# Attention over a long cache on one core: ScalarE's sums in a loop over quarter blocks, VectorE's sums twelve keys at a time

## The chip, the cores and the metric

The kernel runs on one core of one Trainium2 chip. The metric is the device time of one execution in microseconds, median of three runs. The program uses five engines: TensorE (PE, matrix products), VectorE (DVE), ScalarE (ACT), GpSimd (POOL, at the start alone) and SyncE (SP, which issues nearly all loads), and the 16 DMA engines that bring the caches from HBM.

## What is computed

One decoding step: one query token, 16 heads of width 256, and caches of 65536 keys and values per head in bf16. The caches are 1074 MB of the 1084 MB that are read. Cut to what matters:

```python
xn = _layernorm(x)                       # x: [1, 1, 448]
q = (xn @ wq) as [16 heads, 256]
scores = einsum("bhqd,bhkd->bhqk", q, k_cache) * 256 ** -0.5
p = softmax(scores)
o = einsum("bhqk,bhkd->bhqd", p, v_cache)
s = o as [1, 4096] @ wo
g = silu(silu(xn @ w1) @ w2)
out = x + s * g
```

## The kernel before

A head's cache is cut into 4 blocks; a block is 128 keys on each of 128 partitions, 32768 bf16 numbers (64 KB) per partition, 8.39 MB in all. There are 64 blocks. Three buffers R[0], R[1], R[2] take them in turn: the keys of block i are loaded, multiplied by the query in place, and when their scores are copied out, the values of the same block are loaded over them.

```python
KB = 128          # keys per partition in a block
SUB = 32          # a quarter block
ND = 19           # keys of a quarter that VectorE sums; ScalarE sums the other NA = 13
NR = 3
...
R = [pool.tile([P, KW], bf16, name=f"R{t}") for t in range(NR)]
...
def take(e, s, k=1):                      # wait for a semaphore, and count it down
    e.wait_ge(s, k).then_inc(s, -k)
...
def load_k(i, s, h=None):
    if h is not None:
        take(sp, h)                       # TensorE is done with half of the old values
    take(sp, vf[s])                       # ... and with all of them
    sp.dma_start(out=R[s][:, :], in_=block(Kd, i)).then_inc(kl[s], 16)
    sp.sem_inc(kq[s], 16)
    sp.sem_inc(kh[s], 16)

def load_v(i, s):
    take(sp, kf[s])                       # the scores of this block are copied out
    sp.dma_start(out=R[s][:, :], in_=block(Vd, i)).then_inc(vl[s], 16)
```

VectorE multiplies ScalarE's 13 keys of a quarter in one instruction, then does its own 19 by a fused multiply-and-sum each. After four quarters it copies the scores and takes their maximum.

```python
def dve_block(s, between=None):
    def end(c0, c1, own):
        take(dve, pf, (c1 - c0) // SUB)   # ScalarE's quarters are done
        take(dve, sd, own)
        dve.tensor_copy(out=S2[:, c0:c1], in_=S[:, c0:c1]).then_inc(kf[s], 1)
        dve.reduce_max(out=rmax[:, :], in_=S[:, c0:c1], axis=AX.X).then_inc(rm, 1)
        if c0 == 0 and between:
            between()
        dve_gmax()
    take(dve, qr)
    dve.tensor_copy(out=qcur[:, :], in_=ps_q).then_inc(sd, 1)
    halves = between is not None          # the last block: two halves, each with a maximum
    take(dve, kl[s], 16)
    for k in range(NSTEP):                # NSTEP = 4
        ...
        m = dve.tensor_tensor(out=pair, in0=pair, in1=qcur[...broadcast...], op=ALU.mult)
        m.then_inc(mr, 1)
        for j in range(ND):
            c = k * SUB + j
            ins = dve.tensor_tensor_reduce(out=Kv[:, c, :], in0=Kv[:, c, :], in1=qcur[:, :],
                op0=ALU.mult, op1=ALU.add, accum_out=S[:, c : c + 1], ...)
        ...
```

ScalarE adds up the products by an identity activation with an accumulator, keeps the outputs of an earlier block between the second and the third quarter, and does the exponentials. Its loop has a body of three blocks, written out.

```python
def act_sums(s, k):
    take(act, mr)
    for j in range(NA):
        c = k * SUB + ND + j
        prod = R[s][:, c * Dh : (c + 1) * Dh]
        ins = act.activation(out=prod, in_=prod, func=ACT.Identity, accum_out=S[:, c : c + 1])
    ins.then_inc(pf, 1)

def act_block(i, s):
    for k in range(NSTEP):
        if k == NSTEP // 2:
            act_keep(i - 2)               # waits for the products of values two blocks back
        act_sums(s, k)
    act_softmax(i, s)                     # exp into PV[s]
```

TensorE takes the row maximum across partitions, then multiplies the weights by the values of the block before:

```python
def pe_block(i, s):
    pe_turn()
    pe_max(i)
    pe_v(s)
```

The three engines' loops begin at a fixed place of an instruction block (`addr_align`, slot 128 for VectorE and ScalarE, 0 for TensorE and SyncE) and carry a hint for the branch back. The last block is written out behind the loops; there the last values and wo are loaded in pieces.

Of the kernel before, what the change touches and what calls it, by code (L numbers as in the profile page):

```python
# [7 lines left out]
ACT = mybir.ActivationFunctionType  # L8
# [5 lines left out]

KB = 128
SUB = 32
ND = 19
NR = 3


@with_exitstack
def kernel(
# [28 lines left out]
    N1 = H1 * NB  # L51
    NL = NENT - N1
    NSTEP = KB // SUB
    NA = SUB - ND
    DF = D // P
    assert D == DF * P + P // 2
    HP = H // 2
# [13 lines left out]

    KW, HK = KB * Dh, KB // 2

    R = [pool.tile([P, KW], bf16, name=f"R{t}") for t in range(NR)]
    qcur = pool.tile([P, Dh], bf16, name="qcur")
    q8 = pool.tile([HP, 2 * Dh], bf16, name="q8")
    S = pool.tile([P, KB], fp32, name="S")
    S2 = pool.tile([P, KB], fp32, name="S2")
    PV = [pool.tile([P, KB], bf16, name=f"PV{t}") for t in range(NR)]
    rmax = pool.tile([P, 1], bf16, name="rmax")  # L80
    gmax = pool.tile([1, 1], bf16, name="gmax")
    O = pool.tile([2, 2 * Dh], fp32, name="O")
# [61 lines left out]
    def mark(e, ins):  # L144
        count[e] += 1
        ins.then_inc(line[e], 1)
        return (e, count[e])
# [7 lines left out]
    def sem(name):  # L155
        return tc.alloc_semaphore(name)

    def take(e, s, k=1):
        e.wait_ge(s, k).then_inc(s, -k)  # L159
# [11 lines left out]
    rm, tm, gm, bm, pv = sem("rm"), sem("tm"), sem("gm"), sem("bm"), sem("pv")  # L171
    od, oc, ho = sem("od"), sem("oc"), sem("ho")
    sd, sa = sem("sd"), sem("sa")
    dl = {n: sem(f"dl_{n}") for n in ("x", "wq", "w1", "w2", "out")}

    def cuts(*c):
# [47 lines left out]
        dve.reduce_max(out=gmax[0:1, :], in_=ps_m[0:1, :], axis=AX.X).then_inc(gm, 1)  # L224


    def dve_block(s, between=None):
        Kv = R[s][:, :].rearrange("p (c d) -> p c d", d=Dh)


        def end(c0, c1, own):
            take(dve, pf, (c1 - c0) // SUB)
# [4 lines that stand above are left out]
                between()  # L237
            dve_gmax()

        take(dve, qr)  # L240
        dve.tensor_copy(out=qcur[:, :], in_=ps_q).then_inc(sd, 1)  # L241
        halves = between is not None
        take(dve, kl[s], 16)
        for k in range(NSTEP):
            if k == 1:
                take(dve, kq[s], 16)
            if k == NSTEP // 2:
                take(dve, kh[s], 16)
            pair = Kv[:, k * SUB + ND : (k + 1) * SUB, :]
            m = dve.tensor_tensor(  # L250
                out=pair,
                in0=pair,
                in1=qcur[:, None, :].to_broadcast([P, NA, Dh]),
                op=ALU.mult,
            )
            if k == 0:
                m.wait_op(sd, 1, "sem-ge")
            m.then_inc(mr, 1)
            for j in range(ND):
                c = k * SUB + j  # L260
                ins = dve.tensor_tensor_reduce(  # L261
                    out=Kv[:, c, :],
                    in0=Kv[:, c, :],
                    in1=qcur[:, :],
                    scale=1.0,
                    scalar=0.0,
                    op0=ALU.mult,
                    op1=ALU.add,
                    accum_out=S[:, c : c + 1],
                )  # L270
            if k == NSTEP - 1:
                ins.then_inc(sd, 1)
                end(KB // 2 if halves else 0, KB, 1 if halves else 2)
            elif halves and k == NSTEP // 2 - 1:
                ins.then_inc(sd, 1)
                end(0, KB // 2, 2)

    def act_sums(s, k):
        take(act, mr)
        for j in range(NA):  # L280
            c = k * SUB + ND + j
            prod = R[s][:, c * Dh : (c + 1) * Dh]
            ins = act.activation(  # L283
                out=prod,
                in_=prod,
                func=ACT.Identity,
                accum_out=S[:, c : c + 1],
            )
        ins.then_inc(pf, 1)

    def act_softmax(e, s, c0=0, c1=KB):
        def col(a, b):
            return hist[:, at(e + 2), a:b].rearrange("p o s -> p (o s)")

        take(act, bm)
        act.mul(out=col(0, 1), in_=ps_nb, mul=-scale).then_inc(sa, 1)  # L296
        take(act, sa)
        act.activation(  # L298
            out=PV[s][:, c0:c1],
            in_=S2[:, c0:c1],  # L300
            func=ACT.Exp,
            bias=col(0, 1),
            scale=scale,
            accum_out=col(1, 2),
        ).then_inc(pv, 1)
# [5 lines left out]
    def act_keep(e):  # L311
        act_out()
        return act_row(e)

    def act_row(e):
        take(act, ho)
        return act.copy(out=hist[:, at(e + 2), 2:4].rearrange("p o s -> p (o s)"), in_=ps_t)  # L317


    def act_block(i, s):  # L320
        for k in range(NSTEP):
            if k == NSTEP // 2:
                act_keep(i - 2)
            act_sums(s, k)
        act_softmax(i, s)


    def pe_keys(po, t, s, k0, k1, start, stop, done=None):
# [77 lines left out]

    def loop(g, a, b, step, block, more=0, slot=0):
        es, name = {g.engine}, f"passes_{nc.next_id()}"  # L410
        head, ann, body, rest, join, tail = (
            f"{name}_{x}" for x in ("head", "ann", "body", "rest", "join", "tail")
        )
        assert (b - a) % step == 0 and more < step
        last = b if more else b - step
        r = nc.alloc_registers(f"{name}_i", engines=es)
        nc.regs_mov(r, a)
        g.addr_align(bass.FETCH_BLOCK_INSTRUCTIONS, offset=slot, max_nops=0)
        nc.br(head, engines=es)

        def go(lo, hi):
            i = nc.snap(r, min_val=a, max_val=last)
            for s in range(lo, hi):
                block(i + s, s)

        with nc.body(head, valid_engines=es):
            g.br_eq(r, last, on_true=body, on_false=ann)
        with nc.body(ann, valid_engines=es):
            hint = g.mark_branch_hint_location()
            nc.br(body, engines=es)  # L430
        with nc.body(body, valid_engines=es):
            go(0, more or step)
            if more:
                g.br_eq(r, last, on_true=join, on_false=rest)
            else:
                nc.br(join, engines=es)
        if more:
            with nc.body(rest, valid_engines=es):
                go(more, step)
                nc.br(join, engines=es)  # L440
        with nc.body(join, valid_engines=es):
            nc.regs_alu(r, r, step, op=mybir.AluOpType.add)
            g.br_lt(r, last + 1, on_true=head, on_false=tail).branch_hint(hint)
        nc.switch_bb(tail)

    with tc.tile_critical():

        act.dma_start(out=x_f[0:1, :], in_=A_x[0, 0:1, :]).then_inc(dl["x"], 16)
        load_rows(w1_t, B_w1, F, dl["w1"])
# [164 lines left out]
        for s in range(1, NR):  # L614
            load_k(NR + s, s, vh[s])
            load_v(NR + s - 1, s - 1)
        with nc.Fori(2 * NR, LAST - 2, NR, engines={ET.SP}, head_slot={ET.SP: 0}) as i:
            for s in range(NR):
                load_k(i + s, s, vh[s])
                load_v(i + s - 1, (s - 1) % NR)  # L620
# [23 lines left out]
        load_wo(4)  # L644


        loop(dve, 0, LAST, NR, lambda i, s: dve_block(s), slot=128)
        loop(act, 0, LAST, NR, act_block, slot=128)


        def none(p):
# [8 lines left out]
        none(ps_t2).then_inc(ho, 1)  # L660
        need("pe", t9)
        pe_max(0)
        loop(pe, 1, NBLK - 3, NR, pe_block, more=1)
        pe_turn()
        pe_v(1, 96, lambda: pe_max(NBLK - 2))


        def weights(e0, e1, h0, h1, p_tot):
            b = (e1 - e0) // (h1 - h0)
            neg = hist[:, e0 + 2 : e1 + 2, 0]  # L670

# [3 lines left out]
            def spread(T):  # L675
# [4 lines left out]
                out=negM[:, h0:h1], in_=v(neg), axis=AX.X, op=ALU.min  # L680
            ))
            need("dve", t)
            t = mark("dve", dve.tensor_tensor(
                out=v(wgt[:, e0:e1]), in0=spread(negM), in1=v(neg), op=ALU.subtract
            ))
            need("act", t)
            t = mark("act", act.activation(out=wgt[:, e0:e1], in_=wgt[:, e0:e1], func=ACT.Exp))
            need("dve", t)
            t = mark("dve", dve.tensor_tensor(
                out=cf[:, e0:e1], in0=wgt[:, e0:e1], in1=p_tot[0], op=ALU.mult  # L690
            ))
# [32 lines left out]


        def first_heads():
            weights(0, N1, 0, H1, (ps_tot[:, 0:N1], t_s))
            outputs(0, N1, 0, H1, NB)
            mark("dve", dve.tensor_copy(out=OT[:, :, 0:H1], in_=OT32[:, :, 0:H1]))

# [10 lines left out]
            return ins  # L741

        t_s = pe_sums(ps_tot[:, 0:N1], 0, N1)
        act_out()
        pe_turn()
        act_sums(0, 0)
        act_row(LAST - 2)
        act_sums(0, 1)
        dve_block(0, between=first_heads)
        t_o = ("dve", count["dve"])  # L750


# [11 lines left out]
        keys(psO, 2, 2, vn, nl, 2, 3, False)  # L764
        pe_bcast()
        keys(psO, 2, 2, vn, nl, 3, 4, False, od)
        act_softmax(LAST, 0, 0, HK)
        act_sums(0, 2)
        act_out()
        act_sums(0, 3)  # L770
        act_row(LAST - 1)


# [9 lines left out]
        pe_rows()  # L783
        project(h0 + 2, h1)
        pe_bcast()
        act_softmax(LAST + 1, 0, HK, KB)
        pe_turn()
        take(pe, pv)
        t15 = pe_sums(ps_m[:, 0:NL], N1, NENT)
# [67 lines left out]
```

## Time and profile before

| | before |
|---|---|
| time, median of 3 runs | 2519.83 us (2519.68 to 2520.15) |
| span of the profiled run | 2518.0 us |
| bytes read from HBM | 1084.3 MB, 431 GB/s over the span |
| VectorE busy | 2233.4 us, 10277 instructions |
| ScalarE busy | 1446.0 us, 6996 instructions |
| TensorE busy | 1147.2 us |

A profile page gives each engine's busy time, the span in 40 slices (a digit is the busy share in tenths, with the rate of the loads below), the DMA queues, and groups of instructions: line, engine, operation, output and inputs with their shapes, count, total and mean time, and the idle time ahead of them with what ended it. In a timeline a row is start, duration, engine, line, operation. "L283 ACT ACTIVATE" with "ACTIVATION_READ_ACCUMULATOR" is one of ScalarE's sums; "L261 DVE CUSTOM_DVE_ANT_0" with its accumulator read is one fused multiply-and-sum of VectorE; "ACTq" and "DVEq" are waits that the engine's sequencer does alone.

### The profile page before, as it was taken

How to read it: one execution, taken by the hardware profiler on the slowest of the kernel's cores; microseconds unless marked ns; L12 is line 12 of the kernel's file. 1: busy time of each engine (PE TensorE's matmuls, PEld its weight loads, DVE VectorE, ACT ScalarE, POOL GpSimd, SP SyncE). 2: the span in 40 equal slices, each digit the busy share in tenths (PEclk: the TensorE clock that was granted, in tenths of full speed). 3: DMA queues.
4: the chain of work that ended last, by engine and by line, in shares of the span. 5: the costliest groups of instructions: out<-in, count | busy, mean ns of one | idle time of the engine just before them, and what ended most of it. 6: DMA issues, size and time to landing. Idle time of an engine off the chain costs nothing. (4 is left out here: it accounts for less than half of the span.)

```text
span 2518.0 us, 29489 instructions
## 1 busy us (share of the span) xinstructions
PE 1147.2 (46%) x4738; PEld 437.0 (17%) x4738; DVE 2233.4 (89%) x10277; ACT 1446.0 (57%) x6996; POOL 1.9 (0%) x14
## 2 busy tenths in 40 slices
PE   3253543534535435345354353453543534535457
PEld 1121211211112112112111121111111211211122
DVE  6979889889898898898998988989989889889897
ACT  4656556556565565565655655655556556556564
POOL 0000000000000000000000000000000000000000
PEclk7676766767667677677676776776776767767679
DMA  9999999999999999999999999999999999999998
GB/s 422 426 440 420 432 435 431 435 433 433 433 433 433 433 433 433 433 433 433 433 433 433 433 433 433 433 433 433 433 433 434 434 433 433 434 435 436 433 427 357
DMA packets 23316, 1084.47 MB, mean 431 GB/s; under 512 B 2434, under 2 KB 4612, under 8 KB 4996
## 3 DMA queue, kind: packets, MB, share of 16 engines
q1 hardware_dynamic: 23298, 1084.30, 99.7%
q8 instruction: 4, 0.07, 0.0%
q14 instruction: 12, 0.10, 0.0%
q10 hardware_dynamic: 2, 0.00, 0.0%
HBM read 1084.29 MB, written 0.00 MB: 431 GB/s over the span
## 5 line engine op out<-in xcount | busy, mean ns | idle before, releaser
L283 ACT ACTIVATE R<-R 128x256 bf16<-128x256 bf16 x3328 | 1330.8, 401 | 747.5 <-ACTq L159 747.5
L261 DVE CUSTOM_DVE_ANT_0 R<-R,qcur 128x256 bf16<-128x256 bf16 x4864 | 1700.3, 418 | 0.0
L330 PE MATMUL bank<-R,PV 128*2 128x512 bf16 x4096 | 1027.1, 417 | 29.6 <-DMA R<-in_A_v_cache_dram 11.5
L250 DVE TENSOR_TENSOR R<-R,qcur 128x3328 bf16<-128x3328 bf16 x256 | 482.8, 1886 | 190.1 <-DVEq L159 190.0
L283 ACT ACTIVATION_READ_ACCUMULATOR R<-R 128x1 f32 x3328 | 620.9, 187 | 0.0
L342 PE MATMUL bank<-ident,rmax 128*1 128x128 bf16 x65 | 17.1, 263 | 1076.8 <-PEq L159 1076.8
L330 PEld LDWEIGHTS bank<-R,PV 128*2 128x2 bf16 x4096 | 366.0, 90 | 662.4 <-issue 212.9
L261 DVE DVE_READ_ACCUMULATOR2_ANT S<- 128x1 f32 x4864 | 387.1, 80 | 0.0
L342 PEld LDWEIGHTS bank<-ident,rmax 128*1 128x1 bf16 x65 | 5.2, 79 | 1081.1 <-issue 1081.0
L359 PE MATMUL bank<-eye,O 2*128 2x2 f32 x264 | 40.0, 252 | 232.2 <-PEq L159 232.2
L296 ACT ACTIVATE hist<-bank 128x1 f32 (+1 forms) x65 | 11.1, 171 | 199.5 <-ACTq L159 199.5
L359 PEld LDWEIGHTS bank<-eye,O 2*128 2x128 f32 x264 | 36.2, 206 | 249.5 <-issue 249.5
L224 DVE TENSOR_REDUCE gmax<-bank 1x1 bf16<-1x128 f32 x65 | 18.3, 281 | 37.2 <-DVEq L159 37.2
L309 ACT COPY O<-bank 2x512 f32<-2x512 f32 x67 | 37.4, 559 | 21.6 <-ACTq L159 21.6
L317 ACT COPY hist<-bank 128x2 f32 (+1 forms) x66 | 10.5, 159 | 59.9 <-ACTq L159 59.9
L241 DVE CAST qcur<-bank 128x256 bf16<-128x256 f32 x64 | 27.2, 424 | 19.0 <-DVEq L159 19.0
L298 ACT ACTIVATE PV<-S,hist 128x128 bf16<-128x128 f32 (+1 forms) x65 | 26.0, 400 | 13.4 <-ACTq L159 13.1
L373 PE MATMUL bank<-q,ident 8*128 (+1 forms) x63 | 24.3, 386 | 7.7 <-issue 1.3
L234 DVE COPY S<-S 128x128 f32<-128x128 f32 (+1 forms) x65 | 14.7, 226 | 10.4 <-DVEq L159 1.1
L235 DVE TENSOR_REDUCE rmax<-S 128x1 bf16<-128x128 f32 (+1 forms) x65 | 18.1, 279 | 0.0
L348 PE MATMUL bank<-gmax,ones_row 1*128 1x1 bf16 x65 | 10.3, 159 | 4.5 <-PEq L159 0.6
L298 ACT ACTIVATION_READ_ACCUMULATOR PV<-S,hist (+1 forms) x65 | 12.1, 186 | 0.0
(68 smaller groups left out, 90.6 us busy)
## 6 DMA issues: line engine op xcount, KB each, us to landing
R<-in_A_k_cache_dram SPq DMA_DIRECT2D x7, 4096.0 KB, 27.3
R<-in_A_v_cache_dram SPq DMA_DIRECT2D x6, 2048.0 KB, 22.4
R<-in_A_k_cache_dram SPq DMA_DIRECT2D x2, 2048.0 KB, 20.1
R<-in_A_wq_dram SPq DMA_DIRECT2D x1, 3072.0 KB, 12.8
R<-in_A_v_cache_dram SPq DMA_DIRECT2D x3, 1024.0 KB, 25.0
R<-in_A_wo_dram SPq DMA_DIRECT2D x2, 1120.0 KB, 21.8
R<-in_B_w_dram SPq DMA_DIRECT2D x1, 1568.0 KB, 25.7
R<-in_B_w_dram SPq DMA_DIRECT2D x1, 1344.0 KB, 5.8
```

What stands on the lines that cost most here:

```text
L224: dve.reduce_max(out=gmax[0:1, :], in_=ps_m[0:1, :], axis=AX.X).then_inc(gm, 1)
L235: dve.reduce_max(out=rmax[:, :], in_=S[:, c0:c1], axis=AX.X).then_inc(rm, 1)
L241: dve.tensor_copy(out=qcur[:, :], in_=ps_q).then_inc(sd, 1)
L250: m = dve.tensor_tensor(out=pair, in0=pair, in1=qcur[:, None, :].to_broadcast([P, NA, Dh]), op=ALU.mult,)
L261: ins = dve.tensor_tensor_reduce(out=Kv[:, c, :], in0=Kv[:, c, :], in1=qcur[:, :], scale=1.0, scalar=0.0, op0=ALU.mult, op1=ALU.add, accum ...
L283: ins = act.activation(out=prod, in_=prod, func=ACT.Identity, accum_out=S[:, c : c + 1],)
L298: act.activation(out=PV[s][:, c0:c1], in_=S2[:, c0:c1], func=ACT.Exp, bias=col(0, 1), scale=scale, accum_out=col(1, 2),).then_inc(pv, 1)
L309: act.copy(out=O[:, :], in_=po).then_inc(oc, 1)
L330: ins = pe.matmul(po, lhsT=PV[t][:, c : c + 2], rhs=R[s][:, c * Dh : (c + 2) * Dh], start=(start and c == k0), stop=(stop and c == k1 - 2),)
L342: pe.matmul(ps_m[0:1, :], lhsT=rmax[:, 0:1], rhs=ident[:, :], start=True, stop=True).then_inc(tm, 1)
L359: ins = pe.matmul(ps_t2[:, 2 * a : 2 * a + 2], lhsT=Ov[:, j, a, :], rhs=eye2[:, j, :], start=(j == 0), stop=(j == 1), is_transpose=True,)
L373: pe.matmul(ps_q, lhsT=ident[0:HP, at(j)].to_broadcast([HP, P]), rhs=q8[:, o : o + Dh] if isinstance(o, int) else q8[:, bass.ds(o, Dh)], s ...
```

## The change

It shares a quarter of 32 keys out anew. ScalarE sums 18 of them instead of 13. VectorE sums 14: 2 by the fused instruction and 12 by one multiply of 12 keys and one reduction that gives 12 sums (in the last block 6 and 8). The buffers R and PV become parts of one tile each, so that ScalarE can reach any of them by an address in a register, and its loop, with one quarter as its body, walks through all blocks, the last too, with branches to what a quarter needs besides. The fixed places of VectorE's, ScalarE's and SyncE's loops are given up; TensorE's stays. It is meant to make the loops' code short and to unload VectorE.

```diff
-ND = 19
+MIX, MIXL = (2, 12), (6, 8)
+NA = SUB - sum(MIX)
...
-    R = [pool.tile([P, KW], bf16, name=f"R{t}") for t in range(NR)]
+    RR = pool.tile([P, NR * KW], bf16, name="R")
+    R = [RR[:, t * KW : (t + 1) * KW] for t in range(NR)]
...
-            m = dve.tensor_tensor(... [P, NA, Dh] ..., op=ALU.mult)
+            c0, c1, c2, c3 = k * SUB, k * SUB + nt, k * SUB + nt + nr, (k + 1) * SUB
+            m = times(c2, c3)
...
+            times(c1, c2).then_inc(sd, 1)
+            own += 1
+            for c in range(c0, c1):
+                dve.tensor_tensor_reduce(
...
+            ins = dve.tensor_reduce(
+                out=S[:, c1:c2], in_=Kv[:, c1:c2, :], axis=AX.X, op=ALU.add
+            )
+            ins.wait_op(sd, own, "sem-ge")
...
-    def act_sums(s, k):
+    def act_sums(b, c0):
         take(act, mr)
-        for j in range(NA):
-            c = k * SUB + ND + j
-            prod = R[s][:, c * Dh : (c + 1) * Dh]
+        for c in range(SUB - NA, SUB):
+            prod = RR[:, bass.ds(b + c * Dh, Dh)]
             ins = act.activation(
                 out=prod, in_=prod, func=ACT.Identity,
-                accum_out=S[:, c : c + 1],
+                accum_out=S[:, bass.ds(c0 + c, 1)],
             )
...
+    def act_steps():
...
+        with nc.body(body, valid_engines=es):
+            act_sums(
+                nc.snap(rb, min_val=0, max_val=end - SUB * Dh),
+                nc.snap(rc, min_val=0, max_val=KB - SUB),
+            )
+            add(rb, SUB * Dh)
+            add(rc, SUB)
+            g.br_lt(ri, LAST, on_true=norm, on_false=last)
+        with nc.body(norm, valid_engines=es):
+            g.br_eq(rc, HK, on_true=keep, on_false=more)
...
-        with nc.Fori(2 * NR, LAST - 2, NR, engines={ET.SP}, head_slot={ET.SP: 0}) as i:
+        with nc.Fori(2 * NR, LAST - 2, NR, engines={ET.SP}) as i:
...
-        loop(dve, 0, LAST, NR, lambda i, s: dve_block(s), slot=128)
-        loop(act, 0, LAST, NR, act_block, slot=128)
+        loop(dve, 0, LAST, NR, lambda i, s: dve_block(s, MIX))
+        act_steps()
...
-        loop(pe, 1, NBLK - 3, NR, pe_block, more=1)
+        loop(pe, 1, NBLK - 3, NR, pe_block, more=1, slot=0)
...
-        act_sums(0, 0)
-        act_row(LAST - 2)
-        act_sums(0, 1)
-        dve_block(0, between=first_heads)
+        dve_block(0, MIXL, between=first_heads)
```

(The lines with "..." inside them are joined for print. The exponential of the first heads' weights, which ScalarE does in the middle of the last block, now stands in its loop too, with two semaphores of its own.)

## The prediction

> **What bounds the kernel now.** I read the page's shares first, then its slices and its table of DMA queues.
>
> ```profile
> PE 1147.2 (46%) x4738; PEld 437.0 (17%) x4738; DVE 2233.4 (89%) x10277; ACT 1446.0 (57%) x6996; POOL 1.9 (0%) x14
> ...
> GB/s 422 426 440 420 432 435 431 435 433 433 433 433 433 433 433 433 433 433 433 433 433 433 433 433 433 433 433 433 433 433 434 434 433 433 434 435 436 433 427 357
> ...
> q1 hardware_dynamic: 23298, 1084.30, 99.7%
> q8 instruction: 4, 0.07, 0.0%
> q14 instruction: 12, 0.10, 0.0%
> ```
>
> VectorE's 89% tempts, but one load queue keeps all 16 DMA engines at work for 99.7% of the span, and from slice 9 to slice 30 the rate stands at 433 GB/s. In the DMA records that is 433.5, so 1084.3 MB need 2501.3 us. The span is 2518.0, and the other 16.7 us are start (2.0 before the first packet), end (some 5 after the last load's packet) and about 9 of slower stretches: the first 100 us, 200 to 260 us, and the last 80 with their small rows of wo. Nothing on an engine can save more than a few of these. A block of 128 keys per partition is 2 x 8.39 MB, 38.7 us of DMA; 64 of them make the kernel.
>
> So what matters is whether loads are issued before the queue runs dry. SyncE's timeline in the late steady state:
>
> ```profile
> 2301.66 0.33 SPq L207 DMA_DIRECT2D R<-in_A_v_cache_dram  x1
> 2319.11 0.33 SPq L201 DMA_DIRECT2D R<-in_A_k_cache_dram  x1
> 2340.47 0.33 SPq L207 DMA_DIRECT2D R<-in_A_v_cache_dram  x1
> ```
>
> The V load goes out when VectorE has copied the block's scores (the copy of L234, which VectorE's timeline has at 2301.28); the K load already in the queue begins to land at 2305.07 in the landing records. The V load is thus 3.4 us early, the K load (2319.11 against 2324.42) 5.3 us. Those margins are what the change may spend for nothing.
>
> VectorE inside one such block, from its timeline:
>
> ```profile
> 2301.28 0.23 DVE L234 COPY S<-S 128x128 f32<-128x128 f32 x1
> 2301.43 0.28 DVE L235 TENSOR_REDUCE rmax<-S 128x1 bf16<-128x128 f32 x1
> 2302.26 0.28 DVE L224 TENSOR_REDUCE gmax<-bank 1x1 bf16<-1x128 f32 x1 [0.56 <-DVEq L159]
> 2302.78 0.42 DVE L241 CAST qcur<-bank 128x256 bf16<-128x256 f32 x1 [0.23 <-DVEq L159]
> 2306.26 1.89 DVE L250 TENSOR_TENSOR R<-R,qcur 128x3328 bf16<-128x3328 bf16 x1 [3.06 <-DVEq L159]
> ```
>
> VectorE waits 3 us for keys before every block: DMA sets the pace. First multiply to score copy is 33.7 us (2306.26 to 2339.99). The costs of the pieces, from the groups:
>
> ```profile
> L283 ACT ACTIVATE R<-R 128x256 bf16<-128x256 bf16 x3328 | 1330.8, 401 | 747.5 <-ACTq L159 747.5
> L261 DVE CUSTOM_DVE_ANT_0 R<-R,qcur 128x256 bf16<-128x256 bf16 x4864 | 1700.3, 418 | 0.0
> ...
> L250 DVE TENSOR_TENSOR R<-R,qcur 128x3328 bf16<-128x3328 bf16 x256 | 482.8, 1886 | 190.1 <-DVEq L159 190.0
> L283 ACT ACTIVATION_READ_ACCUMULATOR R<-R 128x1 f32 x3328 | 620.9, 187 | 0.0
> ```
>
> They overlap: in the timelines one fused multiply-and-sum starts 0.346 us after the last, one ScalarE sum 0.398 us after the last, and the multiply of 13 keys occupies 1.80 of its 1.89 us.
>
> [...] 3328 elements in 1886 ns are 0.52 ns each plus 153 fixed, and reductions of 64 and 128 (216 and 281 ns) give 1.02 ns per element plus 150. [...] No fetch repeats with the loops here: 16 instruction packets in all. [...]
>
> **The change part by part.** *VectorE, a steady quarter of 32 keys.* Before: 1.80 + 19 x 0.346 = 8.37 us. After: multiply of 18 keys, 4608 x 0.52 + 153 - 85 = 2.47; multiply of 12, 1.67; two fused sums, 0.69; one reduction of 3072 elements at 1.02 ns + 150 - 85, 3.20. Sum 8.03, so 0.34 less, 1.4 us a block. The saving comes from the five keys handed to ScalarE; product and reduction of 12 keys (4.87) cost more than 12 fused sums would (4.15). VectorE's dependent reduction is covered by the two fused sums ahead of it.
>
> *ScalarE.* 18 sums a quarter instead of 13: 17 x 0.398 + 0.49 = 7.26 us, of 9.7 us that DMA allows. Each now has register addresses. ScalarE's sequencer records show the price where it already pays it, at L296, L298 and L317: one fused register operation of 46 to 69 ns, and the engine starts 171 to 181 ns after the wait instead of 87. So some 90 ns of sequencer time per sum, perhaps twice that for two registers. A branch operation runs while the exponential is still executing, so the sequencer runs ahead; a sum that takes 0.398 us hides it. The accumulator written through a register at L298 takes 186 ns, as with a fixed address. I leave the pitch at 0.398.
>
> *The block.* ScalarE can start a quarter 2.77 us after VectorE does (2.55 multiply, 0.12 wake-up as before, 0.1 registers). Quarter ends, from the block's first multiply: 10.0, 18.1; then the keep of output and row (1.7 us between sums, from 1005.95 to 1007.63 in its timeline), so 27.1; then 34.4. VectorE is done at 32.2. ScalarE now ends the block, and the score copy comes at 34.5 instead of 33.7. Both margins of the loads shrink by 0.8 us, to about 2.6 and 4.5: still positive, so a steady block stays 38.7 us. Gain and loss there: zero.
>
> *Start.* The same sum for the first blocks puts score copies at about 58.0, 94.3, 133.0 and 169.7 us (now 56.72, 92.21, 128.91, 164.81); the third is late because ScalarE, which in this block waits till 116.47 for the first outputs, then has 36 sums of work instead of 26. V loads leave at about 94.6, 133.2, 170.0 and 212.1 against first landings of 96.5, 135.3, 174.0 and 212.7. The last is tight (0.6 us; now 1.4). I charge 0.3 us.
>
> *End.* In the last block (6 fused, 8 reduced) VectorE needs 7.83 us a quarter, but ScalarE starts late (its output copy waits until about 2462) and does 36 sums before the half's maximum: first half at 2477.4 instead of 2475.47, second at 2498.9 instead of 2495.62. The loads of the end are queued well ahead and don't notice. On TensorE, 1.5 of these 3.3 us vanish: the row maximum is ready at 2495.95 now but TensorE takes it at 2497.53, after older products. So the last softmax is 1.8 us later, and the timeline of TensorE shows how much the last loads absorb:
>
> ```profile
> 2500.28 2.05 PE L734 MATMUL bank<-R,OT 128*1 128x448 bf16 x10
> 2502.17 1.89 PE L330 MATMUL bank<-R,PV 128*2 128x512 bf16 x8
> 2504.30 1.89 PE L330 MATMUL bank<-R,PV 128*2 128x512 bf16 x8 [0.25 <-DMA R<-in_A_v_cache_dram]
> 2506.78 3.61 PE L330 MATMUL bank<-R,PV 128*2 128x512 bf16 x16 [0.59 <-DMA R<-in_A_v_cache_dram]
> ```
>
> TensorE waits twice for V pieces. Started 1.8 us later without waits, the 42 products end at 2510.9 instead of 2510.2: +0.6 us.
>
> *SyncE's alignment.* Its loop is short, and after its branch it waits some 10 us for the next buffer (2302.1 to 2311.9 in its records); zero. Sum: 2519.8 + 0.3 + 0.6 = 2520.7.
>
> **The rivals.** *ScalarE becomes the bound.* A block of its own would be 72 sums, 1.7 for the keep, 4.8 from its last sum through the copy, the next query (1.5 us later) and the first multiply. 38.7 - 6.5 over 72 is 0.447 us a sum. If register work lifts the pitch above that, every 10 ns cost 0.72 us a block, some 43 us in all; a pitch of 0.47 gives about 2620. For it: two addresses on two registers, each perhaps with its own operation. Against it: two of 90 ns plus a dispatch of at most 0.25 us (13 sums go out in 3.3 us at 2461 to 2465, with the engine's queue in the way) make 0.43.
> *Instruction fetch.* The loops lose alignment, and ScalarE's its hint. A 16 KB instruction packet takes 1.0 to 1.1 us in the records; one per quarter would eat the margins and cost up to 1 us a block, 2580. Against it: ScalarE's loop body is some 100 instructions instead of 200, VectorE's 130 instead of 300.
> *The end is worse.* If VectorE's and ScalarE's handshake for the first heads' weights takes longer, or sums start later, each us goes straight onto the end: 2523.
> *It gains.* If the start's slow stretches (1.4 us between 200 and 260) close, 2518. There is no mechanism I can see for more.
>
> **Range and chances.** Steady state has a floor, so most weight lies within 3 us of 2520.7; the tail upward is for the two rivals. Eight in ten: 2518 to 2525. Faster by over 2% would need 50 us under a floor of 2501: 0.005. Slower by over 2%: 0.025.
>
> **What would show it.** VectorE busy some 80 us less, ScalarE's about 510 us more (1280 sums x 0.398), 78%; 433 GB/s in the middle slices; sums still 0.398 us apart; the score copy waiting for ScalarE for about 2 us in each block, 34.5 us after the first multiply; V loads landing about 23.0 us after issue (23.8 now), K loads 24.7 (25.5 now); fewer or no DMA waits in TensorE's last products. I am wrong if the pitch of the sums grows, if middle slices fall below 433, or if the instruction queues grow with the loop.

## The result and the profile after

The changed kernel takes 2560.03 us (median; 2556.93 to 2561.74) against 2519.99 us: a ratio of 1.0157, 95% interval 1.0142 to 1.0171. That is 40 us more. That is still within 2%, the likeliest of the three outcomes predicted, but far outside the predicted range of 2518 to 2525.

The shares, the rates by slice and the queues of the kernel after, from its page:

```profile
PE 1156.8 (45%) x4738; PEld 439.7 (17%) x4738; DVE 2159.7 (84%) x2117; ACT 1949.4 (76%) x9556; POOL 1.9 (0%) x14
...
GB/s 419 428 438 427 427 425 426 424 423 433 424 426 421 429 430 426 425 432 420 425 426 426 425 424 419 439 425 423 429 423 427 424 415 434 426 432 428 426 422 325
...
q1 hardware_dynamic: 23298, 1084.30, 99.1%
...
q14 instruction: 4, 0.03, 0.0%
```

The level stretch of 433 GB/s is gone. The queue is still "busy" for 99.1% of the span, so this share hides the loss. From 300 to 2380 us, summed over the DMA records, the rate is 426.3 GB/s (433.3 before). In that stretch two things grew, both counted as time of all 16 engines: time without any packet, from 0.1 to 10.8 us, and the excess of 64 KB packets over their usual 2.42 us, from 2.0 to 26.0 us (911 packets took over 2.5 us, 29 before). Together 34.7 us. The median block repeats after 39.15 us instead of 38.70, and the mean one after 39.36.

The rest is at the end. From the last packet of the last load to the end of the span it is 11.37 us; before it was 5.86. So 34.7 + 5.5 = 40.2 of the 40.6 us by which the two spans (2518.0 and 2558.6) differ.

The costliest groups of the kernel after, different shapes apart:

```profile
L298 ACT ACTIVATE R<-R x4608 | 1840.0, 401 | 354.3 <-ACTq L162 354.2
...
L298 ACT ACTIVATION_READ_ACCUMULATOR R<-R x4608 | 862.2, 187 | 0.0
L282 DVE TENSOR_REDUCE S<-R 128x12 f32<-128x3072 bf16 x252 | 843.2, 3346 | 0.0
L247 DVE TENSOR_TENSOR R<-R,qcur 128x4608 bf16<-128x4608 bf16 x256 | 652.6, 2549 | 158.3 <-DVEq L162 158.1
L247 DVE TENSOR_TENSOR R<-R,qcur 128x3072 bf16<-128x3072 bf16 x252 | 441.0, 1750 | 0.0
```

ScalarE's sum with register addresses takes the same 401 and 187 ns as with fixed ones, and VectorE's three kinds of work cost what was predicted. No instruction became dear.

The end of a block on VectorE, and SyncE's load issues around it, in the middle of the kernel after (columns: start, length, engine, line, operation, and in brackets the idle time ahead with what ended it):

```profile
1307.01 3.35 DVE L282 TENSOR_REDUCE S<-R 128x12 f32<-128x3072 bf16 x1
1312.72 0.23 DVE L239 COPY S<-S 128x128 f32<-128x128 f32 x1 [2.37 <-DVEq L162]
```

```profile
1274.44 0.33 SPq L211 DMA_DIRECT2D R<-in_A_v_cache_dram  x1
1291.28 0.33 SPq L205 DMA_DIRECT2D R<-in_A_k_cache_dram  x1
1313.20 0.33 SPq L211 DMA_DIRECT2D R<-in_A_v_cache_dram  x1
1331.12 0.33 SPq L205 DMA_DIRECT2D R<-in_A_k_cache_dram  x1
1353.67 0.33 SPq L211 DMA_DIRECT2D R<-in_A_v_cache_dram  x1
```

VectorE is done and waits 2.37 us for ScalarE before it may copy the scores (before: 0.15 us after its own last sum). The copy frees the K buffer, and SyncE sends the V load 0.5 us later. The landing records put the first of the 16 landings of the K load ahead at 1274.67, 1315.23 and 1354.09. The V loads were therefore 0.23, 2.03 and 0.42 us early; the first and the last of these are among the three smallest of the run. I call this distance the lead. Its median over the steady blocks is 1.84 us (a tenth of the loads below 0.77), where the kernel before has 3.33 (2.86).

### The profile page after: what moved, and what is told of

The parts are those of the page before. It is cut to its first block, busy times and chain, and to the rows that moved or that the text cites. A ratio compares the mean times of both kernels' runs of the same rounds, so it can differ in the third digit from the quotient of the medians.

```text
span 2558.6 us, 30100 instructions
## 1 busy us (share of the span) xinstructions
PE 1156.8 (45%) x4738; PEld 439.7 (17%) x4738; DVE 2159.7 (84%) x2117; ACT 1949.4 (76%) x9556; POOL 1.9 (0%) x14
## 3 DMA queue, kind: packets, MB, share of 16 engines
q1 hardware_dynamic: 23298, 1084.30, 99.1%
## 5 line engine op out<-in xcount | busy, mean ns | idle before, releaser
L298 ACT ACTIVATE R<-R x4608 | 1840.0, 401 | 354.3 <-ACTq L162 354.2
L247 DVE TENSOR_TENSOR R<-R,qcur 128x4608 bf16<-128x4608 bf16 (+1 forms) x512 | 1077.6, 2145 | 158.3 <-DVEq L162 158.1
L298 ACT ACTIVATION_READ_ACCUMULATOR R<-R x4608 | 862.2, 187 | 0.0
L282 DVE TENSOR_REDUCE S<-R 128x12 f32<-128x3072 bf16 (+1 forms) x256 | 852.3, 3329 | 0.0
L272 DVE CUSTOM_DVE_ANT_0 R<-R,qcur 128x256 bf16<-128x256 bf16 x528 | 200.7, 417 | 0.0
L272 DVE DVE_READ_ACCUMULATOR2_ANT S<- 128x1 f32 x528 | 42.5, 80 | 0.0
L313 ACT ACTIVATE PV<-S,hist 128x128 f32 (+1 forms) x65 | 26.0, 400 | 14.7 <-ACTq L162 14.4
L355 PE MATMUL bank<-gmax,ones_row 1*128 1x1 bf16 x65 | 10.3, 159 | 4.6 <-PEq L162 0.6
```

Of the source, the lines that this page charges most:

```text
L247: return dve.tensor_tensor(out=keys, in0=keys, in1=qcur[:, None, :].to_broadcast([P, c1 - c0, Dh]), op=ALU.mult,)
L282: ins = dve.tensor_reduce(out=S[:, c1:c2], in_=Kv[:, c1:c2, :], axis=AX.X, op=ALU.add)
L313: act.activation(out=pv_out, in_=S2[:, c0:c1], func=ACT.Exp, bias=col(0, 1), scale=scale, accum_out=col(1, 2),).then_inc(pv, 1)
```

## The experiments

Theory A: ScalarE now ends the block, the score copy and the V load come later, and with so small a lead the DMA engines run short of queued packets around each V load. The rivals: B, the register loop on ScalarE disturbs something by itself; C, VectorE's long reductions and multiplies slow the DMA packets; D, the lost alignment of the loops.

The diffs show only the lines that matter. In the runs without a reduction, its multiply and the wait for it are left out too, and VectorE's loop is aligned as before.

**The register loop with the old division (B).** All sums of VectorE fused, 13 on ScalarE, as before; the loop of ScalarE is the new one, in the last block too, and VectorE's loop is aligned as before.

```diff
-MIX, MIXL = (2, 12), (6, 8)
+MIX, MIXL = (19, 0), (19, 0)
```

> The loop of the changed kernel with the old shares: ScalarE sums 13 keys by register addresses in the one loop, VectorE 19 by fused sums, no reduction. Theory A (the V load leaves too late, because ScalarE's 18 sums end the block later): score copy 33.7 us after the first multiply, V load 3.3 us ahead of the first landing of the keys before it, 433 GB/s, 2520 us within 2. Rival B (ScalarE's register loop and its branches hold something up): 2555 to 2565. Rival C (reductions and wider products of VectorE slow the packets): 2520, so C is not told from A here.

Measured 2520.43 us, ratio 1.0001 [0.9992, 1.0009]; copy 33.73 us after the first multiply, V lead 3.24, 433.2 GB/s. The loop costs nothing, and B falls.

**Less work on ScalarE, the rest as after (C).** ScalarE leaves out the last 4 of its 18 sums in each quarter (those scores stay zero), so the time is that of less work.

```diff
-        for c in range(SUB - NA, SUB):
+        for c in range(SUB - NA, SUB - 4):
+        gp.memset(S[:, :], 0.0)     # once, at the start
```

> The changed kernel, but ScalarE leaves out the last 4 of its 18 sums of each quarter (their scores stay 0, the work is left out); VectorE's products of 18 and 12 keys and its reductions are all there. Theory A: ScalarE is done before VectorE, score copy 32.4 to 32.7 us after the first multiply, V load over 4 us early, 433 GB/s, 2517 to 2521 us. Rival C: VectorE's work is unchanged, so packets stay slow, 2550 to 2560. Rival B: 2550 to 2560.

Measured 2516.18 us, ratio 0.9984 [0.9977, 0.9991]. VectorE's products and reductions are all there; its V lead is 3.31 us and the middle runs at 433.5 GB/s:

```profile
GB/s 423 427 440 432 432 431 433 434 434 433 433 434 434 434 432 435 433 434 434 434 434 434 434 434 434 434 434 434 434 434 434 434 434 434 434 434 434 434 428 365
```

So C falls: the same VectorE work beside the same loads costs no bandwidth once ScalarE is done in time. One expectation failed, though: the score copy came 0.72 us sooner than before, at 33.01, but the V lead did not grow to over 4 us.

**Alignment (D).** After, with VectorE's loop and SyncE's loop aligned as before.

```diff
+        with nc.Fori(2 * NR, LAST - 2, NR, engines={ET.SP}, head_slot={ET.SP: 0}) as i:
+        loop(dve, 0, LAST, NR, lambda i, s: dve_block(s, MIX), slot=128)
```

> The changed kernel with the fixed places of VectorE's and SyncE's loops given back. Theory A: no change, 2555 to 2563 us. Rival D (branches out of an instruction block cost the loops time): back to 2520 to 2530.

Measured 2560.92 us, ratio 1.0165 [1.0148, 1.0182]: as after. D falls.

**The delay alone (A).** The kernel before, with nothing but a memset on VectorE ahead of each score copy. Three lengths: 480, 1000 and 2050 elements.

```diff
+            if not between:
+                dve.memset(dum[:, 0:1000], 0.0).then_inc(sd, 1)
+                own += 1
             take(dve, pf, (c1 - c0) // SUB)
```

> The kernel before, with one fill of 1000 elements (about 1.1 us) on VectorE ahead of each steady block's score copy, and nothing else of the change. Theory A: copy at 34.8 us, V lead down to between 1 and 2.5 us, packets near the V issue slow, engines idle there, 424 to 428 GB/s in the middle, 2550 to 2565 us. Rivals B, C and D: 2520 to 2522, since a lead above zero is enough.

The memset was meant to take 1.1 us and took half: it executed as half as many 32-bit words. The delay was 0.53 us, so this run became a middle dose: 2538.04 us, 1.0075 [1.0058, 1.0092]. The other two:

> The kernel before with a fill of 2050 bf16 ahead of each steady score copy. In the last such run 1000 bf16 were filled as 500 words in 0.475 us and put the copy off by 0.53 us (33.73 to 34.26), so this should put it off by 1.1 us, to 34.8, where the changed kernel has it. Theory A (only the lateness of the V load counts): the whole loss of the change without any of its parts, 2555 to 2565 us, V lead about 1.8 us, over 800 slow packets. If something else in the change adds to it: 2535 to 2550.

> The kernel before with a fill of 480 bf16 (240 words, some 0.25 us) ahead of each steady score copy: copy at 34.0, V lead 2.9 us. Theory A with a soft edge near 3 us: 2524 to 2531. If the loss is in proportion to the delay with no edge (33 us per us of delay, as from 0 to 0.53): 2528. If the edge lies below 2.9: 2520 to 2521.

Measured 2556.42 us, 1.0144 [1.0127, 1.0160], for a delay of 1.08 us, and 2522.62 us, 1.0011 [1.0003, 1.0018], for 0.26. The groups of these memsets, in the runs with the long, the middle and the short one:

```profile
L234 DVE MEMSET dum<- 128x1025 uint32 x63 | 57.5, 912 | 10.4 <-issue 10.4
```

```profile
L234 DVE MEMSET dum<- 128x500 uint32 x63 | 29.9, 475 | 3.4
```

```profile
L234 DVE MEMSET dum<- 128x240 uint32 x63 | 16.3, 258 | 0.0
```

The rates of the run with the long memset:

```profile
GB/s 419 425 441 416 428 425 431 423 429 426 427 426 427 428 427 420 429 432 426 427 428 426 427 422 418 429 429 428 429 424 433 428 419 434 425 427 422 424 426 355
```

The kernel with the long memset has the old ScalarE program, the old VectorE work and the old end; its copy comes at 34.81 us, where the changed kernel has 34.82. It loses 36 of the 40 us, and in the middle 35.0 against 36.8 (table below), which leaves some 2 us for everything else that the change does there. A is shown as to the late V load; why a short lead slows the packets stays open (below). And the price is not in proportion: 0.26 us of delay cost 2.6 us in all, 0.53 cost 18, 1.08 cost 36. From one step to the next that is some 10, then 57, then 33 us for each us of delay added. The smallest of the three is none of the sums that I had written down (2520 to 2521, 2524 to 2531, or 2528), and with runs from 2519.97 to 2528.85 its cost is only just told from nothing.

**Is it the V loads only?** Spare one-column products of TensorE ahead of the release of each V buffer delay the K loads: 12 of them, then 76.

```diff
+        for _ in range(12):      # 76 in the second run
+            pe_mark()
         pe_mark().then_inc(vf[s], 1)
```

> The kernel before with 12 more one-column products on TensorE ahead of the release of a value buffer: the K load, not the V load, leaves later, by 1 to 2 us. Its lead is 5.0 us and stays at 3 us or more. Theory A (a lead of some 3 us is what is needed, whichever load it is): 2520 to 2523. Rival (any lateness of a load costs a share of it): some 33 us per us, 2550 or more.

> The kernel before with 76 one-column products more ahead of the release of each V buffer (12 took 0.28 us off the lead of the K loads, so 76 take some 1.8 us: about 5.0 to 3.2 us); the V loads' lead stays 3.3 us. Theory A (about 3 us of lead is enough for either load) expects 2520 to 2524 us and a rate of 433 GB/s in the middle. A rival, that every us taken off any lead costs something, from the V loads' slope (18 us for 0.8 us of lead), expects 2545 or more. If TensorE itself becomes late with the extra products, the score copy's lead to the V load shows it.

Twelve took only 0.28 us from the K lead (4.99 to 4.71) and the time stayed, 2520.25 us, 1.0003 [0.9994, 1.0012]: too small a dose to decide anything. With 76 the median K lead is 2.97 us (a tenth below 1.94), the score copy still comes at 33.73, and the time is 2537.72 us, 1.0073 [1.0056, 1.0090]. That is neither number that I had written down. "About 3 us is enough" was too generous for a median: a lead of 3 in the median leaves half the loads below it. The rival slope was too steep. Of the loss in the middle, 9.3 us lie around K loads and 8.7 around V loads, whose leads the late K loads made uneven (3.13, a tenth below 2.42).

**The new division on ScalarE, in time, and the new last block.** The kernel after, with 14 fused sums and no reduction in a steady quarter, so that VectorE's quarter is shorter and ScalarE's 18 register sums end in time; the last block as changed. It parts the steady state from the end.

```diff
-MIX, MIXL = (2, 12), (6, 8)
+MIX, MIXL = (14, 0), (6, 8)
```

> The kernel after with 14 fused sums and no reduction in a steady quarter (ScalarE keeps its 18 sums in the register loop), and the changed last block as it is (6 fused, 8 reduced). VectorE's quarter is then about 7.4 us, and ScalarE ends the block at about 33.8 us after the first multiply, as VectorE did before. It parts the steady state from the end. Theory A: V lead 3.1 to 3.3 us, 433 GB/s in the middle, and what is left over 2520 us is the price of the new end: 2523 to 2524 if that is the 3.6 us by which the kernel after exceeds the delayed kernel with the old end, 2520.6 if it is the predicted 0.6. Rival (18 register sums a quarter cost DMA time by themselves, whatever the lead): 2550 or more.

Measured 2526.74 us (2524.19 to 2539.82 over 11 runs), 1.0037 [1.0025, 1.0049]. In the profile the copy comes at 34.04, V lead 3.24, middle 432.8 GB/s: 18 sums in the register loop are free when the lead is kept, apart from some 3 us where it was not (a tenth of the leads below 2.53). I had expected 2523 to 2524 us; the further 3 us are about this loss in the middle. The last load's packet ends 2.0 us later than before, and from there to the end it is 10.34 us instead of 5.86: the changed last block costs 4.5 us by itself.

**The other direction.** Sixteen sums on each engine, in the changed kernel and in the old one.

```diff
-MIX, MIXL = (2, 12), (6, 8)
+MIX, MIXL = (16, 0), (16, 0)
```

```diff
-ND = 19
+ND = 16
```

> The changed kernel's loop with 16 sums on ScalarE and 16 fused sums on VectorE a quarter, no reduction. Worked out: VectorE 7.73 us a quarter, ScalarE's last quarter ends 32.3 us after the first multiply, so the copy comes at about 32.5. Theory A: V lead 3.5 to 4.5 us, 433.5 GB/s, no loss; start and end better than before as with the sums left out, 2515 to 2519 us.

> The kernel before with 16 fused sums on VectorE and 16 on ScalarE in every quarter, instead of 19 and 13; nothing else. A multiply of 16 keys and 16 fused sums make a VectorE quarter of about 7.8 us, ScalarE's 16 sums 6.5: the score copy moves to some 32.4 us after the first multiply. Theory A: V lead 3.3 us or more, middle at 433 GB/s, nothing gained there as DMA is at its floor; 2517 to 2520 us with the shorter start and end, as the register loop with the same division has (2518.6). If the register loop itself costs or saves anything, the two differ by more than 1 us.

Measured 2518.56 us, 0.9994 [0.9985, 1.0002], and 2518.43 us, 0.9992 [0.9983, 1.0001]. The copy comes at 32.47 and 32.36 us, more than a us sooner than before, and the middle stays at 433.4 and 433.5 GB/s. The leads did not grow with it, against what I had expected (3.5 to 4.5, and 3.3 or more): they are 3.33 and 3.14 us. A sooner score copy gains nothing in the middle, and the register loop costs nothing against the fixed one. If these two kernels are faster at all, it is by some 1.5 us; the intervals just include 1.

**All runs together.** Copy: median us from a block's first multiply to its score copy. Lost: engines without packets plus excess of slow packets from 300 to 2380 us, in us of all 16 engines. Tail: last load's last packet to the end of the span. Leads, losses and tails are from the landing and packet records of each profile.

| kernel | copy | V lead, median / lowest tenth | K lead | lost | tail | time |
|---|---|---|---|---|---|---|
| before | 33.73 | 3.33 / 2.86 | 4.99 | 2.1 | 5.9 | 2520.0 |
| register loop, 13 sums | 33.73 | 3.24 / 3.14 | 4.89 | 3.1 | 5.8 | 2520.4 |
| 16 and 16, register loop | 32.47 | 3.33 / 3.22 | 4.98 | 1.5 | 5.8 | 2518.6 |
| 16 and 16, old loop | 32.36 | 3.14 / 2.86 | 4.82 | 1.3 | 5.8 | 2518.4 |
| after, 4 sums left out | 33.01 | 3.31 / 3.29 | 5.07 | 1.2 | 5.7 | 2516.2 |
| delay 0.26 | 33.99 | 3.27 / 2.47 | 4.84 | 4.4 | 5.8 | 2522.6 |
| delay 0.53 | 34.26 | 2.50 / 1.94 | 4.42 | 16.1 | 5.8 | 2538.0 |
| delay 1.08 | 34.81 | 1.96 / 1.08 | 4.13 | 35.0 | 5.8 | 2556.4 |
| K delay, 12 products | 33.73 | 3.36 / 2.93 | 4.71 | 2.6 | 5.8 | 2520.2 |
| K delay, 76 products | 33.73 | 3.13 / 2.42 | 2.97 | 18.5 | 5.8 | 2537.7 |
| 18 sums in time, new end | 34.04 | 3.24 / 2.53 | 4.84 | 5.0 | 10.3 | 2526.7 |
| after, aligned | 34.82 | 1.82 / 1.20 | 4.07 | 37.0 | 11.5 | 2560.9 |
| after | 34.82 | 1.84 / 0.77 | 3.98 | 36.8 | 11.4 | 2560.0 |

Lost and tail together, against the row of before, give the time column to within 1.5 us, but for three rows that miss by 3 to 4 us. The profiled execution of the middle delay was some 5 us shorter than the median of that kernel; the long delay had a slower first 300 us (423.5 GB/s; 426.2 before), the kernel with sums left out a faster one (428.5).

The same records, load by load over all thirteen kernels that have a profile: the loss from 3 us before to 8 us after the issue of a load, by that load's lead.

| lead, us | V loads | lost per V load, us | K loads | lost per K load, us |
|---|---|---|---|---|
| below 0.5 | 3 | 1.44 | | |
| 0.5 to 1 | 15 | 1.12 | | |
| 1 to 1.5 | 24 | 0.86 | | |
| 1.5 to 2 | 61 | 0.66 | 7 | 0.49 |
| 2 to 2.5 | 86 | 0.41 | 11 | 0.33 |
| 2.5 to 3 | 108 | 0.12 | 15 | 0.16 |
| 3 to 3.25 | 93 | 0.03 | 22 | 0.11 |
| 3.25 to 3.5 | 290 | 0.01 | 21 | 0.08 |
| 3.5 and more | 4 | 0.01 | 610 | 0.01 |

This is the curve that the prediction lacked. K and V loads lie on nearly the same one: next to nothing is lost from 3 us (V) or 3.5 us (K) up, some 0.1 us at 2.5 to 3, and about 0.5 us more for each further us that is missing.

A lead at its usual size does not tell how much can be spent. Where the copy comes at 32.47, 33.01, 33.73, 33.99 and 34.04 us, the 16 landings of a K load lie 2.31, 1.77, 1.06, 0.84 and 0.81 us apart in the median, and the V lead stays at 3.24 to 3.33: a later copy goes with a narrower spread. Only past that does the lead fall, to 2.50 us at a copy of 34.26. Why the spread follows the copy is not shown.

## Why the prediction was wrong

**What bounds the kernel: right, and this is why it could lose.** DMA sets the pace (its load queue is busy for 99.7% of the span before and 99.1% after), and what its engines lose goes onto the time: the 34.7 us lost in the middle and the 5.5 at the end are 40.2 of the 40.6 us between the spans.

**VectorE, ScalarE, loop: right.** VectorE busy 74 us less (predicted 80), ScalarE 503 more (510), 76% (78%). The multiplies of 4608 and 3072 elements took 2549 and 1750 ns, which is 0.52 ns an element plus 152, and the reduction 3346, a quarter some 8.1 us (8.03); the sums stay 0.398 us apart. Each sum shows one fused register operation of 74 to 79 ns in ScalarE's sequencer records, hidden as supposed. Instruction packets fell from 12 to 4 in queue q14 and stayed at 4 in q8, so the rival of instruction fetch is out, and the pitch rival too.

**The block's end: right in mechanism, 0.3 us short.** The copy came at 34.82 us instead of the predicted 34.5, 2.37 us after VectorE's last operation.

**The step that failed.** "Both margins of the loads shrink by 0.8 us, to about 2.6 and 4.5: still positive, so a steady block stays 38.7 us. Gain and loss there: zero." The size was off: the V margin shrank by 1.5 us, to 1.84. Of this, 1.1 is the later copy. The remaining 0.4 goes with a wider spread of the landings, partly made up by the longer block: the 16 landings of a K load now lie 2.20 us apart in the median instead of 1.06. The lead is measured to the first of them, but VectorE waits for the last one before it starts. The main error is in the criterion. I took any margin above zero as free. It is free only above some 3 to 3.5 us. Even the predicted 2.6 would have cost 0.1 us a block on the curve, and a spread of leads around it more: the run with a median lead of 2.50 lost 18 us. The kernel before stood near the edge already: 0.26 us of delay doubled its loss in the middle, from 2.1 to 4.4 us, so "what the change may spend for nothing" was less than 0.3 us, not 3.4.

The evidence was in the trace of before: at 211.34 and 250.32 us V loads left 1.4 and 2.1 us ahead of the first landing, and the DMA records show 416.7 GB/s from 200 to 220 us and 426 from 240 to 260. I had seen the slow stretch and charged 0.3 us for it in the start, without asking what a lead of this size would cost 60 times over. Among the rivals, margins appear only where instruction fetch would use them up; a loss at a positive margin was no rival at all.

Landing time says the same: V loads land 23.9 us after issue, where I predicted 23.0 (23.8 before), and K loads 25.7, where I predicted 24.7 (25.5 before). I had taken it that a load issued 0.8 us later lands after a time shorter by as much; here these times grew by 0.1 and 0.2 us.

**Start: right.** Copies at 57.68, 94.26, 132.35 and 169.33 us (predicted 58.0, 94.3, 133.0, 169.7). The V load that I called tight left at 211.41, 1.46 us early instead of 0.6.

**A sum that was wrong.** Faster by over 2% means below 2469 us, which is some 32 us under the floor of 2501, not 50. The argument does not hang on it.

**End: predicted +0.6 us, measured +5.5 on the tail.** The term was mis-sized in two places. TensorE's timeline from the last row maximum on, first of the kernel before, then of the kernel after:

```profile
2496.78 0.92 PE L734 MATMUL bank<-R,OT 128*1 128x448 bf16 x4
2497.53 0.22 PE L342 MATMUL bank<-ident,rmax 128*1 128x128 bf16 x1
...
2510.40 0.54 PE L734 MATMUL bank<-R,OT 128*1 128x448 bf16 x2
```

```profile
2532.68 0.92 PE L817 MATMUL bank<-R,OT 128*1 128x448 bf16 x4
2536.46 0.22 PE L349 MATMUL bank<-ident,rmax 128*1 128x128 bf16 x1 [2.86 <-PEq L162]
...
2539.40 3.89 PE L817 MATMUL bank<-R,OT 128*1 128x448 bf16 x10
2543.09 7.91 PE L337 MATMUL bank<-R,PV 128*2 128x512 bf16 x32
2550.84 0.54 PE L817 MATMUL bank<-R,OT 128*1 128x448 bf16 x2
```

Measured from the last load's last packet (2512.13 and 2547.22), the row maximum comes 14.60 us ahead of it before and 10.76 after: 3.8 us later, not 1.8, with TensorE waiting 2.86 us for it. Most of the missing 2 us arise where ScalarE's sums of the last block start: the copy of outputs ahead of them, which I put 0.7 us later than before (2462 against 2461.27), comes 2.6 us later (2499.00), measured the same way. The DMA waits in the products did vanish as predicted, but the stretch from the row maximum to the last two products grew from 12.9 to 14.4 us instead of shrinking. The reason is in the windows of the two kernels over the ten products and the 32 (columns: window, length, busy time and count of the five engines, granted TensorE clock, DMA share, GB/s):

```profile
2500.20:2502.20 2.00, 2.00 (x13) 0.93 (x13) 1.36 (x7) 0.68 (x3) 0.00 (x0) 1.00 0.99 414
2502.20:2510.40 8.20, 7.36 (x33) 2.34 (x31) 3.79 (x4) 0.00 (x0) 0.00 (x0) 1.00 0.89 342
```

```profile
2539.30:2543.00 3.70, 3.70 (x11) 1.30 (x12) 3.01 (x8) 0.68 (x3) 0.00 (x0) 0.50 1.03 397
2543.00:2551.00 8.00, 8.00 (x34) 2.94 (x33) 2.14 (x4) 0.00 (x0) 0.00 (x0) 0.89 0.26 95
```

The granted clock is 0.50 in the first of the after windows and 1.00 in the same stretch before, so ten products take 3.89 us instead of 2.05. The run with the new end and a sound steady state shows the same (row maximum 2.7 us later against the last load, 14.5 us from it to the last two products; in the aligned kernel after 5.3 and 13.1):

```profile
2502.24 0.22 PE L351 MATMUL bank<-ident,rmax 128*1 128x128 bf16 x1 [2.69 <-PEq L162]
...
2505.18 3.89 PE L819 MATMUL bank<-R,OT 128*1 128x448 bf16 x10
2508.87 8.02 PE L339 MATMUL bank<-R,PV 128*2 128x512 bf16 x32
```

The kernel with four sums left out has the same last block on VectorE and TensorE, but no such wait. Its clock stays at 1.00 there, and the stretch takes 12.1 us, shorter than before as I had predicted:

```profile
2494.91 0.22 PE L349 MATMUL bank<-ident,rmax 128*1 128x128 bf16 x1
...
2507.05 0.54 PE L818 MATMUL bank<-R,OT 128*1 128x448 bf16 x2
```

The clock records of the kernels before and after hold these two levels alone, 0.50 and 1.00. By such records the half clock lasts 6.83 us after, 6.83 with the new end and a sound steady state, and 3.41 in the aligned kernel; the longer half clock goes with the longer stretch (14.4, 14.5 and 13.1 us). That the wait is what lowered the clock is argued from these kernels and not tested alone. A single wait does not settle it: 2.23 us at 2488 us in the kernel before left the clock at 1.00, and 2.14 us at 2485 us in the kernel with sums left out was followed by a stretch of half clock.

**What stays open.** Why about 3 us of lead are needed was not settled. At the start of this kernel the first packet begins 1.0 us after its issue (0.96 to 2.0), which does not make 3 us. Why most of the loss is in slow packets (26.0 us) and less in missing ones (10.8) is not shown either. Nor was it settled what sets the spread of a load's landings: it is 2.31 and 2.68 us in the two 16-and-16 kernels, which lose next to nothing (1.5 and 1.3 us), and 2.20 in the changed kernel, which loses 36.8.

## What to carry to other kernels

In a kernel at the DMA limit, measure for every large load how long before the first landing of the load ahead it is issued, and treat this lead as having a floor (here 3 to 3.5 us), not as slack down to zero; look for stretches of the same trace with smaller leads and read their price there. A lead at the floor can still hide some slack in the spread of the landings (by comparison of the kernels here, under 0.3 us before and over 1 us with 16 and 16 sums); a short delay like the ones above measures it. Moving work to an idle engine is not free when that engine then ends the block, because the block's end frees the buffer that the next load needs (here the copy went from 33.73 to 34.82 us, and the lead from 3.33 to 1.84). And weigh the tail apart: after the last load's last packet every us counted fully here (5.5 of the 40.6 us between the spans), and waits of 2.86 and 2.69 us shortly before it went with half of TensorE's clock (0.50 for 6.83 us).

## What the runs showed of the hardware that was not expected

- A load queue with a busy share of 99.1% ran 1.6% slower than one with 99.7% (426.3 against 433.3 GB/s). Most of the loss is in packets that take longer than 2.42 us (26.0 us, 2.0 before), less in missing ones (10.8 us, 0.1 before).
- The price of a late issue is not in proportion to the delay: 2.6, 18 and 36 us for 0.26, 0.53 and 1.08 us per block.
- With a sooner score copy the lead did not grow; the landings of the load ahead spread instead, from 1.06 us at a copy of 33.73 to 2.31 at 32.47.
- A memset of zeros over 1000 bf16 elements ran as 500 32-bit words in 475 ns, which halved the first delay I had meant to set.
- ScalarE's sum costs 401 and 187 ns whether its addresses are fixed or in registers.
